# Attention's steps reordered: last keys' scores as steps of their own, steps that run one or two periods late, and the scaling of x on GpSimd throughout

## The chip, the cores and the metric

The kernel runs on one core of one Trainium2 chip. The engines of that core run their own instruction streams side by side and meet through semaphores: TensorE (PE; PEld is its weight load), VectorE (DVE), ScalarE (ACT), GpSimd (POOL) and SyncE (SP), which here issues nearly all DMAs. The metric is the device time of one execution in microseconds. Three runs of the kernel before took 1297.23, 1299.07 and 1300.94 us; the median is 1299.07 us.

## The reference

Two blocks follow each other. The first is attention over 8 batches of 8 heads with 576 positions of 64 values, where a score is kept only if it lies within tau of its row's maximum:

```python
scores = scale * np.matmul(q, k.transpose(0, 1, 3, 2))
thresh = np.max(scores, axis=-1, keepdims=True) - tau
scores = np.where(scores >= thresh, scores, -1000000000.0)
scores = scores - np.max(scores, axis=-1, keepdims=True)
attn = np.exp(scores)
attn = attn / (np.sum(attn, axis=-1, keepdims=True) + 1e-09)
return np.matmul(attn, v).astype(np.float32)
```

Its output, turned into 4608 rows of 512 values, is the x of a feed-forward block:

```python
h = np.maximum(x @ w_in, 0.0)
return (h * h @ w_out).astype(np.float32)
```

w_in is 512 x 2048 and w_out is 2048 x 512. Both arrive as 64-bit floats and the kernel converts them to 32 bits on the chip.

## The kernel before

**Stages.** Attention comes first. The feed-forward block follows, with a fast form of matrix product that trades products for sums (the helpers on lines 121 to 133). The two share TensorE's accumulation memory, PSUM: the feed-forward stage opens its own pools there only when attention's are closed. The conversion of the weights and part of the sums on them are spread over attention's periods.

**Units, pairs and periods.** Two heads make a head pair (32 of them). The queries of a head pair are cut into four blocks of 128; the last 64 queries of two head pairs make a ninth unit. That gives 144 units. `period(p)` (line 619) takes two units, A = 2p and B = 2p + 1; the text calls them pair p. There are 72 such pairs. The loop on line 1146 runs the periods one after the other, and each runs the steps of a list in the order in which the list names them. Since the kernel schedules by hand, this order is also the order of each engine's own stream. `CONVERTING` is the list while weights are converted (periods 2 to 34), `PLAIN` the one after that, and `BEGIN_WITH` holds those of periods 0 and 1.

**The steps and their engines.**

| step | what it does, line | engine |
|---|---|---|
| SA, SB | scores of A, of B against the first 512 keys (L434); SA also does the last 64 keys of both units | PE |
| topA0 ... topB1 | copies 128 x 576 scores out of PSUM and takes their extreme (L452) | DVE |
| leastA, leastB | adds tau (L459) | POOL |
| powA0 ... | exponential (L462) | ACT |
| maskA0 ... | threshold, product and row sum (L467) | DVE |
| over, inv | row sum + 1e-9 (L474), reciprocal (L477), for the pair before | POOL, DVE |
| V, W, U | turn the weights of a pair with transposes (L380), in three parts; W also spreads the reciprocals with small products (L515) | PE |
| eV, eW, eU | copy the turned weights to SBUF (L523) | ACT |
| PV | product of values and weights (L532), 72 or 108 instructions | PE |
| x | takes PV out of PSUM (L657 or L659) | ACT or DVE |
| xm | scales x on GpSimd in converting periods (L669), hands the stores of x and the next loads of v to SP | POOL, SP |
| T, eT | turn queries or keys with transposes (L398), copy them (L403, L411), ask for the next loads | PE, ACT, SP |
| fetch, c1 ... c6 | load a block of weights and convert it: L205 (c1), L212 (c2), L219 (c3), L227 (c4), L235 (c5), L245 (c6) | SP, ACT, POOL, POOL, DVE, DVE, POOL |
| s1, s2 | one sum on the weights each (L122, L125) | POOL |

In period p of the old lists, scores, exponentials and masks are those of pair p, V and W turn pair p - 1, U and PV belong to pair p - 2. The table `TURNS` names the periods in which T has something to turn; of the periods 35 to 71 those are 30.

**PSUM.** Six banks (`sc`) hold scores: A's first 512 keys lie in banks 0 and 5, B's in banks 2 and 3, and the last 64 keys of both in banks 1 and 4. T turns into the free middle of banks 1 and 4 (`spots`), W into banks 2 and 3, PV into banks 0 and 5. Two more banks (`pt`) serve U and V.

**Waits.** `touch` (line 355) notes which banks an instruction uses. To each new one it adds a wait for the last instruction of every other engine on the same bank, and it declares that instructions on other banks don't depend on each other, except for the kinds in `MEET` (line 353) whose ring slots coincide. Rings hold three head pairs of turned queries (`Q_RING`), four of turned keys and of the last queries (`K_RING`), and two pairs of turned weights (`W_RING`).

Of the kernel before, what the change touches and what calls it, by code (L numbers as in the profile page):

```python
# [10 lines left out]
FP32 = mybir.dt.float32  # L11
# [37 lines left out]
def kernel(  # L49
# [300 lines left out]
    behind = mybir.DependencyInfo(mybir.DependencyClass.Sync, mybir.DependencyReason.DATA)  # L350

    Q_RING, K_RING, W_RING = 3, 4, 2
    MEET = (("scores", "turned", (Q_RING, K_RING)), ("values", "weights", (W_RING,)), ("x", "weights", (W_RING,)))

    def touch(what, made, at, size, key=0):

# [34 lines left out]
    def turn(i, which, spots, other=None):  # L391

        nat, to = loaded.pop((i, which)), places(i)
        of = [nat[:, t, :] for t in range(FULL)] + ([loaded.pop((i, 2))] if which else [])
        for t, x in enumerate(of):
            for r, (spot, at) in enumerate(spots):
                rows = ds(r * HALF, HALF)
                made = nc.tensor.transpose(spot[:, ts(t, HALF)], x[rows, :], ident[rows, rows])  # L398
                touch("turns", made, at, BANK)
        half = FULL * HALF  # L400

        def scaled(to, spot):
            touch("turned", nc.scalar.activation(out=to, in_=spot[0], func=AF.Identity, scale=qscale[:, :]), spot[1], BANK, i)  # L403

        def then():
            part = lambda r, x, n: (spots[r][0][:, ds(x, n)], spots[r][1])
            if which:
                for r, n in ((0, half), (1, half + REST)):
                    spot = part(r, 0, n)
                    copy_by = other if r and other else nc.scalar.copy  # L410
                    touch("turned", copy_by(to[1][:, ds(r * half, n)], spot[0]), spot[1], BANK, i)  # L411
# [11 lines left out]
    def scores(n, rest):  # L423

        of, t = units[n]
        at_k, count = (MAIN, REST) if rest else (0, MAIN)
        for j in range(2):
            first = n % 2 != j
            to = (3 * j + 1) * BANK + first * (BANK - REST) if rest else (3 * j + 2 * first) * BANK
            for c in range(2):  # L430
                rows, at = ds(j * D, D), ds(c * HALF, HALF)
                qT, kT, qR = turned[of[c]]
                lhs = qT[rows, ds((c * FULL + t) * HALF, HALF)] if t < FULL else qR[rows, :]
                made = nc.tensor.matmul(  # L434
                    sc[at, ds(to, count)], lhs, kT[rows, ds(at_k, count)], start=True, stop=True
                )
                touch("scores", made, to, count, of[c])

    def softmax(n):

        if n % 2 == 0:
            smalls[n // 2] = sb.tile([P, 4, 4], FP32, tag="small", bufs=4, name="small")
        small = smalls[n // 2]
        nmx, thr, sm = (small[:, i, ds(n % 2 * 2, 2)] for i in range(3))
        w = sb.tile([P, CH, 2, D], FP32, tag="w", bufs=4, name="w")
        s = sb.tile([P, 2, S], FP32, tag="s", bufs=2, name="s")
        weights[n] = w
        of = lambda j: s[:, j, :].rearrange("p (c d) -> p c d", d=D)

        def top(j):  # L450
            at = 3 * j * BANK + (n % 2 != j) * (2 * BANK - REST)
            made = nc.vector.tensor_scalar(  # L452
                out=s[:, j, :], in0=sc[:, ds(at, S)], scalar1=1.0, scalar2=None,
                op0=ALU.mult, op1=ALU.min, accum_out=nmx[:, j : j + 1],
            )
            touch("tops", made, at, S)

        def least():
            nc.gpsimd.tensor_scalar(out=thr, in0=nmx, scalar1=tau_p[:, :], scalar2=None, op0=ALU.add)  # L459

        def power(j):
            nc.scalar.activation(  # L462
                out=w[:, :, j, :], in_=of(j), func=AF.Exp, bias=nmx[:, j : j + 1], scale=-1.0
            )

        def mask(j):
            nc.vector.scalar_tensor_tensor(  # L467
                out=w[:, :, j, :], in0=of(j), scalar=thr[:, j : j + 1], in1=w[:, :, j, :],
                op0=ALU.is_le, op1=ALU.mult, accum_out=sm[:, j : j + 1],
            )  # L470
# [88 lines left out]
    def has(n):  # L559
        return 0 <= n < NU  # L560
# [22 lines left out]
    def converts(p):  # L583
        return is_wide and (has_chunk(p) or has_chunk(p - 1))
# [4 lines left out]
    def begun(n):  # L589
        return starts.get(n)  # L590

    PLAIN = """
        SA c3 T topA0 over U eU s1 SB topA1 powA1 leastA topB0 powB0 c1 s2 PV c4 V fetch
        inv powA0 c5 topB1 powB1 eT maskA1 x xm W eV maskA0 leastB c2 c6 eW maskB0
        maskB1
    """.split()
    CONVERTING = """
        fetch SA U eU T SB topA0 s1 c1 topA1 topB0 c3 V PV leastA over powA0 topB1
        powA1 powB0 c4 eT inv x maskA1 maskA0 W leastB maskB0 c5 eV c2 powB1 c6 eW maskB1 xm
    """.split()  # L600

    BEGIN_WITH = {
        0: """
            SA SB fetch topA0 T topA1 leastA topB0 topB1 leastB powA0 powA1 eT powB0 powB1
            maskA0 maskA1 maskB0 maskB1
        """.split(),
        1: """
            fetch SA SB T eT over topA0 topA1 leastA inv V topB0 topB1 leastB powA0 powA1 eV W
            powB0 eW maskA0 maskA1 powB1 maskB0 maskB1
        """.split(),  # L610
    }

# [6 lines left out]
    def period(p):  # L619
# [30 lines left out]
        def values_out():  # L650
            if not has(2 * m):
                return
            late["x"] = x = sb.tile([P, 2, P], FP32, tag="x", bufs=2, name="x")
            for j in range(2):
                from_ = sc[:, ds(5 * j * BANK, P)]
                if converts(p):
                    made = nc.scalar.copy(x[:, j, :], from_)  # L657
                else:
                    made = nc.vector.tensor_tensor(  # L659
                        out=x[:, j, :], in0=from_, in1=wT[m][:, ts(SCALE_AT + j, P)], op=ALU.mult  # L660
                    )
                touch("x", made, 5 * j * BANK, P, m)

        def given_out():
            if has(2 * m):
                x = late.pop("x")
                if converts(p):
                    both = x[:, :, :].rearrange("p j n -> p (j n)")
                    nc.gpsimd.tensor_tensor(out=both, in0=both, in1=wT[m][:, ds(SCALE_AT * P, 2 * P)], op=ALU.mult)  # L669
                wT.pop(m)  # L670
                valued(m)
                give_x(m, x)
            ask(False)

        def scored_a():
            if has(A):
                scores(A, False)
                scores(A, True)
                scores(B_, True)
                softmax(A)  # L680

        def scored_b():
            if has(A):
                scores(B_, False)
                softmax(B_)

        def every(key):
            for then in late.get(key, ()):
# [27 lines left out]

    def inner(product, copy, temp, bank, final, tick):

# [400 lines left out]
    with tc.manual_schedule():  # L1119
        with ExitStack() as stack:  # L1120
# [222 lines left out]
```

## Time and profile before

| | |
|---|---|
| median of three runs | 1299.07 us |
| span of the profiled execution | 1298.2 us |
| granted TensorE clock, mean | 0.997 |
| PE, DVE, ACT, POOL busy | 98%, 78%, 65%, 71% |
| attention, up to the first product of the feed-forward stage | 507.8 us |

The profile is of one execution, and its sums are made against its span of 1298.2 us, which is 0.9 us under the median. A row of the timeline gives the start, the time, the engine and line, the operation, output and input by the program's names, and a count where several like instructions are merged. A bracket at its end names the idle time before it and what ended that. Instructions of one engine overlap in part, so the distance from one start to the next says what an instruction costs its engine, and the time of one says when its result is there.

### The profile page before, as it was taken

The page shows a single profiled execution, that of the slowest core. Times are in us where ns is not written, and L with a number is a line of the kernel's source. Part 1 is how long each engine was busy: PE and PEld are TensorE (multiplying, and loading weights), DVE is VectorE, ACT ScalarE, POOL GpSimd, SP SyncE. Part 2 cuts the span into 40 slices and gives each one's busy share as a digit, 9 for nine tenths or more (in the row PEclk, how much of TensorE's full clock was granted, in tenths as well). Part 3 has the DMA queues.
Part 4 walks back from the last instruction along what each step waited for, and adds up shares of the span by engine and source line. Part 5 has one row for each costly group of instructions (what it writes and reads, how often), then busy time and mean ns, then how long its engine had stood idle before and what let it go on. Part 6 is the DMA issues. An engine that isn't in the chain of part 4 may idle for free.

```text
span 1298.2 us, 45819 instructions
## 1 busy us (share of the span) xinstructions
PE 1276.4 (98%) x18287; PEld 1117.7 (86%) x18287; DVE 1007.0 (78%) x2423; ACT 845.5 (65%) x1498; POOL 926.8 (71%) x1031
## 2 busy tenths in 40 slices
PE   8999999999999999999999999999999999999998
PEld 5777777677777778988888888999999999999998
DVE  6999999999999996886887878867646654665463
ACT  6999999888998984666765856675523432343240
POOL 2787878755555321888897989858787767777775
PEclk8999999999999999999999999999999999999999
DMA  5665566544333312667768768589554224522411
GB/s 143 163 160 154 153 192 180 149 103 110 85 79 80 92 34 64 191 183 218 212 186 226 218 175 235 162 304 391 195 159 164 83 86 159 163 80 88 160 34 34
DMA packets 291413, 196.20 MB, mean 151 GB/s; under 512 B 100096, under 2 KB 252160, under 8 KB 291200
## 3 DMA queue, kind: packets, MB, share of 16 engines
q1 hardware_dynamic: 289888, 192.87, 51.5%
q8 instruction: 144, 2.36, 0.8%
q14 instruction: 69, 0.57, 0.2%
q10 hardware_dynamic: 1312, 0.41, 0.1%
HBM read 120.85 MB, written 72.35 MB: 149 GB/s over the span
## 4 chain that ended last, share of the span: by engine, by line
PE 86%; ACT 5%; DVE 4%; DMA 3%; issue 2%; POOL 0%; SPq 0%; ACTq 0%; DVEq 0%; POOLq 0%
PE po L1077 28%; PE ph L935 16%; PE sc L532 11%; PE sc L434 10%; PE ph L942 10%; PE pt L380 6%; DVE arena L452 2%; PE sc L515 2%; PE sc L398 2%; ACT arena L462 1%; ACT arena L523 1%; DMA g<-arena 1%; PE sc L380 1%; DVE arena L125 1%; DMA wall<-w 1%
## 5 line engine op out<-in xcount | busy, mean ns | idle before, releaser
L125 POOL TENSOR_TENSOR arena<-arena 128x512 f32<-128x512 f32 (+1 forms) x314 | 378.1, 1222 | 147.0 <-DVE arena L125 119.3
L1077 PE MATMUL po<-wall,arena 128*128 128x128 f32 x3528 | 395.0, 275 | 1.9 <-ACT arena L752 1.4
L1077 PEld LDWEIGHTS po<-wall,arena 128*128 128x128 f32 x3528 | 394.4, 192 | 2.5 <-ACT arena L752 1.8
L125 DVE TENSOR_TENSOR arena<-ph,arena 128x512 f32<-128x512 f32 x378 | 255.1, 689 | 79.9 <-PE ph L935 31.5
L122 POOL TENSOR_TENSOR arena<-arena 128x128 f32<-128x128 f32 (+1 forms) x322 | 265.4, 825 | 23.0 <-DMA arena<-w 6.6
L935 PE MATMUL ph<-arena,wall 128*128 128x256 f32 x1176 | 256.6, 380 | 1.8 <-DVE arena L125 1.4
L935 PEld LDWEIGHTS ph<-arena,wall 128*128 128x128 f32 x1176 | 222.2, 190 | 35.9 <-DVE arena L125 5.4
L125 DVE TENSOR_TENSOR arena<-po,arena 128x128 f32<-128x128 f32 x378 | 108.2, 290 | 167.7 <-PE po L1077 163.4
L467 DVE SCALAR_TENSOR_TENSOR arena<-arena 128x576 f32<-128x576 f32 x288 | 235.7, 855 | 0.9 <-ACT arena L462 0.9
L791 ACT COPY c<-arena 128x512 f32<-128x512 f32 (+1 forms) x295 | 169.0, 578 | 71.8 <-DVE arena L122 35.8
L452 DVE TENSOR_SCALAR_CACHE_REDUCE arena<-sc 128x576 f32<-128x576 f32 x288 | 205.1, 748 | 10.9 <-ACT arena L523 4.3
L462 ACT ACTIVATE arena<-arena 128x576 f32<-128x576 f32 x288 | 208.7, 773 | 7.4 <-DVE arena L452 4.2
L532 PEld LDWEIGHTS sc<-arena 64*64 64x64 f32 x5760 | 159.2, 133 | 36.5 <-DVE arena L452 19.8
L532 PE MATMUL sc<-arena 64*64 64x128 f32 (+1 forms) x5760 | 180.5, 262 | 2.9 <-DVE arena L452 1.3
L434 PE MATMUL sc<-arena 64*64 64x64 f32 (+1 forms) x2304 | 176.2, 415 | 3.8 <-ACT arena L403 2.4
L523 ACT COPY arena<-pt 128x1024 f32<-128x1024 f32 x144 | 146.4, 1016 | 27.9 <-PE pt L380 26.5
L122 DVE TENSOR_TENSOR arena<-arena,c 128x512 f32<-128x512 f32 x235 | 154.4, 666 | 11.0 <-ACT c L791 7.6
L752 ACT COPY arena<-po 128x128 f32<-128x128 f32 x63 | 16.6, 264 | 186.4 <-PE po L1077 183.7
L942 PE MATMUL ph<-arena,wall 128*128 128x128 f32 x1176 | 132.0, 275 | 0.7 <-DVE arena L659 0.7
L942 PEld LDWEIGHTS ph<-arena,wall 128*128 128x128 f32 x1176 | 131.6, 192 | 1.1 <-issue 0.8
L380 PEld LDWEIGHTS pt<-ident,arena 64*128 64x128 f32 x2304 | 83.5, 139 | 40.0 <-ACT arena L523 30.1
L434 PEld LDWEIGHTS sc<-arena 64*64 64x64 f32 x2304 | 74.0, 134 | 42.2 <-issue 14.1
(54 smaller groups left out, 1079.7 us busy)
## 6 DMA issues: line engine op xcount, KB each, us to landing
arena<-g SPq DMA_DIRECT2D x144, 256.0 KB, 4.4
g<-arena SPq DMA_DIRECT2D x192, 128.0 KB, 2.9
w<-arena SPq DMA_DIRECT2D x60, 256.0 KB, 2.8
wall<-w SPq DMA_DIRECT2D x49, 256.0 KB, 5.2
g<-arena SPq DMA_DIRECT2D x48, 256.0 KB, 3.8
arena<-w SPq DMA_DIRECT2D x44, 256.0 KB, 3.3
arena<-in_v_dram SPq DMA_DIRECT2D x32, 288.0 KB, 3.8
out_dram<-arena SPq DMA_DIRECT2D x70, 128.0 KB, 2.2
```

Of the source, the lines that this page charges most:

```text
L122: e.tensor_tensor(out=out, in0=x, in1=y, op=ALU.subtract)
L125: e.tensor_tensor(out=out, in0=x, in1=y, op=ALU.add)
L380: made = nc.tensor.transpose(pt[:, r, ts(slot, HALF)], of[rows, :], ident[rows, rows])
L434: made = nc.tensor.matmul(sc[at, ds(to, count)], lhs, kT[rows, ds(at_k, count)], start=True, stop=True)
L452: made = nc.vector.tensor_scalar(out=s[:, j, :], in0=sc[:, ds(at, S)], scalar1=1.0, scalar2=None, op0=ALU.mult, op1=ALU.min, accum_out=nmx ...
L462: nc.scalar.activation(out=w[:, :, j, :], in_=of(j), func=AF.Exp, bias=nmx[:, j : j + 1], scale=-1.0)
L467: nc.vector.scalar_tensor_tensor(out=w[:, :, j, :], in0=of(j), scalar=thr[:, j : j + 1], in1=w[:, :, j, :], op0=ALU.is_le, op1=ALU.mult, a ...
L532: made = nc.tensor.matmul(sc[ds(u * D, D), ds(5 * j * BANK + row, count)], loaded_v[i][rows, (c - (u != j)) % CH, :], wT[m][rows, ds(weigh ...
L791: nc.scalar.copy(c, y)
L935: nc.tensor.matmul(to[:, 2 * j : 2 * j + 2, :], W_IN[m, k][:, ts(2 * h + j, P)], part_x(steps, k, m), start=(not more and j == 0), stop=Tr ...
L942: nc.tensor.matmul(to[:, j, :], W_IN[m, k][:, ts(j, P)], x, start=(not more and j == 0), stop=True, skip_group_check=True,)
L1077: nc.tensor.matmul(to, g[:, j, :], w[:, j, :], start=(not more and j == 0), stop=(j == 3), skip_group_check=True)
```

## The change

- `BEGIN_WITH`, `PLAIN` and `CONVERTING` get new orders. A name may end in one or two dashes: in iteration p it then stands for that step of period p - 1 or p - 2. `step` runs each step of each period once, and the periods of one step in their order; where a list changes, steps already run are left out. The loop runs three iterations longer, for the late steps.
- The scores of the last 64 keys leave SA and become the steps RA and RB.
- x is always copied out of PSUM by ACT, and xm always scales it on GpSimd; DVE's product on line 659 goes.
- `MEET` tells turned queries from turned keys and the last queries' scores from the others, so that each is tested against its own ring.
- The buffers for w and s are found by the unit's number instead of by the order of asking.

```diff
-    MEET = (("scores", "turned", (Q_RING, K_RING)), ("values", "weights", (W_RING,)), ("x", "weights", (W_RING,)))
+    MEET = (("scores", "turnedq", (Q_RING,)), ("scores", "turnedk", (K_RING,)), ("last scores", "turnedk", (K_RING,)), ("values", "weights", (W_RING,)), ("x", "weights", (W_RING,)))
...
-        half = FULL * HALF
+        half, kind = FULL * HALF, "turnedk" if which else "turnedq"
...
-                touch("scores", made, to, count, of[c])
+                touch("scores" if t < FULL else "last scores", made, to, count, of[c])
...
-        if n % 2 == 0:
+        if n // 2 not in smalls:
...
-        w = sb.tile([P, CH, 2, D], FP32, tag="w", bufs=4, name="w")
-        s = sb.tile([P, 2, S], FP32, tag="s", bufs=2, name="s")
+        w = sb.tile([P, CH, 2, D], FP32, tag=f"w{n % 4}", name="w")
+        s = sb.tile([P, 2, S], FP32, tag=f"s{n % 2}", name="s")
...
+    FIRST_PERIOD = -2
     PLAIN = """
-        SA c3 T topA0 over U eU s1 SB topA1 powA1 leastA topB0 powB0 c1 s2 PV c4 V fetch
-        inv powA0 c5 topB1 powB1 eT maskA1 x xm W eV maskA0 leastB c2 c6 eW maskB0
-        maskB1
+        PV-- x-- V-- eV-- RA- c1- c3- inv-- W-- xm-- eW-- powB1-- c2 maskA0-- SA- maskA1-- U- c4 topA0- s1--
+        powB0-- topA1- leastA- SB- eU- maskB1-- c6 RB- T- s2 maskB0-- eT- over- topB0- powA0- topB1- c5
+        powA1- leastB- fetch
     """.split()
     CONVERTING = """
-        fetch SA U eU T SB topA0 s1 c1 topA1 topB0 c3 V PV leastA over powA0 topB1
-        powA1 powB0 c4 eT inv x maskA1 maskA0 W leastB maskB0 c5 eV c2 powB1 c6 eW maskB1 xm
+        RB- maskA0-- SA- maskA1-- inv-- powB1-- W-- U- topA0- eW-- c6- fetch topA1- leastA- SB- maskB0-- c1-
+        c3- eT- maskB1-- topB0- c4 over- topB1- c2- leastB- eU- powA1- powA0- PV- c5 V- x- RA powB0- eV- T
+        xm- s1 s2
     """.split()
...
-            SA SB fetch topA0 T topA1 leastA topB0 topB1 leastB powA0 powA1 eT powB0 powB1
-            maskA0 maskA1 maskB0 maskB1
+        SA RA RB SB fetch topA0 T topA1 leastA topB0 topB1 leastB powA0 powA1 eT powB0 powB1 maskA0 maskA1
+        maskB0 maskB1
...
-                if converts(p):
-                    made = nc.scalar.copy(x[:, j, :], from_)
-                else:
-                    made = nc.vector.tensor_tensor(
-                        out=x[:, j, :], in0=from_, in1=wT[m][:, ts(SCALE_AT + j, P)], op=ALU.mult
-                    )
-                touch("x", made, 5 * j * BANK, P, m)
+                touch("x", nc.scalar.copy(x[:, j, :], from_), 5 * j * BANK, P, m)
...
-                if converts(p):
-                    both = x[:, :, :].rearrange("p j n -> p (j n)")
-                    nc.gpsimd.tensor_tensor(out=both, in0=both, in1=wT[m][:, ds(SCALE_AT * P, 2 * P)], op=ALU.mult)
+                both = x[:, :, :].rearrange("p j n -> p (j n)")
+                nc.gpsimd.tensor_tensor(out=both, in0=both, in1=wT[m][:, ds(SCALE_AT * P, 2 * P)], op=ALU.mult)
...
-        def scored_a():
-            if has(A):
-                scores(A, False)
-                scores(A, True)
-                scores(B_, True)
-                softmax(A)
-
-        def scored_b():
-            if has(A):
-                scores(B_, False)
-                softmax(B_)
+        def scored(n):
+            if has(n):
+                scores(n, False)
+                softmax(n)
+
+        def scored_rest(n):
+            if has(n):
+                scores(n, True)
...
-            "SA": scored_a, "SB": scored_b,
+            "SA": lambda: scored(A), "SB": lambda: scored(B_),
+            "RA": lambda: scored_rest(A), "RB": lambda: scored_rest(B_),
...
+        return steps
+
+    tables, made_steps = {}, set()
+
+    def step(name, p):
+
+        if p < FIRST_PERIOD or (name, p) in made_steps:
+            return
+        step(name, p - 1)
+        made_steps.add((name, p))
+        if p not in tables:
+            tables[p] = period(p)
+        tables[p][name]()
+
+    def run_period(p):
+
         for name in BEGIN_WITH.get(p) or (CONVERTING if converts(p) else PLAIN):
-            steps[name]()
-        for n in (A, B_):
-            if has(n) and units[n][1] == FULL:
-                for i in units[n][0]:
-                    turned.pop(i)
+            step(name.rstrip("-"), p - name.count("-"))
...
-            for p in range(-2, NU // 2 + 3):
-                period(p)
+            for p in range(FIRST_PERIOD, NU // 2 + 6):
+                run_period(p)
```

More of the change, by code (lines that the diff above doesn't have):

```diff
@@ L399, in turn @@
                 touch("turns", made, at, BANK)
-        half = FULL * HALF
+        half, kind = FULL * HALF, "turnedk" if which else "turnedq"
         def scaled(to, spot):
-            touch("turned", nc.scalar.activation(out=to, in_=spot[0], func=AF.Identity, scale=qscale[:, :]), spot[1], BANK, i)
+            touch(kind, nc.scalar.activation(out=to, in_=spot[0], func=AF.Identity, scale=qscale[:, :]), spot[1], BANK, i)
         def then():
@@ L410, in then @@
                     copy_by = other if r and other else nc.scalar.copy
-                    touch("turned", copy_by(to[1][:, ds(r * half, n)], spot[0]), spot[1], BANK, i)
+                    touch(kind, copy_by(to[1][:, ds(r * half, n)], spot[0]), spot[1], BANK, i)
                 scaled(to[2], part(0, half, REST))
@@ L603 @@
         0: """
-            SA SB fetch topA0 T topA1 leastA topB0 topB1 leastB powA0 powA1 eT powB0 powB1
-            maskA0 maskA1 maskB0 maskB1
+        SA RA RB SB fetch topA0 T topA1 leastA topB0 topB1 leastB powA0 powA1 eT powB0 powB1 maskA0 maskA1
+        maskB0 maskB1
         """.split(),
         1: """
-            fetch SA SB T eT over topA0 topA1 leastA inv V topB0 topB1 leastB powA0 powA1 eV W
-            powB0 eW maskA0 maskA1 powB1 maskB0 maskB1
+        fetch SA RA RB SB T eT over topA0 topA1 leastA inv V topB0 topB1 leastB powA0 powA1 eV W powB0 eW
+        maskA0 maskA1 powB1 maskB0 maskB1
         """.split(),
```

## The prediction

> **What bounds the kernel now.** I read the page first, then the busy times of stretches, then the order of TensorE's instructions in single periods, then the other engines beside it. The change touches only the attention stage, so the stretches are cut there: the first covers the converting periods between the first score read of pair 2 and of pair 33 (31 periods), the second the plain periods between those of pair 34 and pair 71 (37 periods), the third the drain up to the last read of attention's PSUM.
>
> ```profile
> PE 1276.4 (98%) x18287; PEld 1117.7 (86%) x18287; DVE 1007.0 (78%) x2423; ACT 845.5 (65%) x1498; POOL 926.8 (71%) x1031
> 22.80:243.50 220.70, 216.86 (x5314) 162.04 (x5312) 219.41 (x588) 212.72 (x381) 174.88 (x215) 1.00 0.62 164
> 250.50:493.70 243.20, 240.02 (x6328) 180.41 (x6322) 234.59 (x704) 217.75 (x339) 120.81 (x171) 1.00 0.36 84
> 493.70:507.60 13.90, 12.00 (x374) 9.94 (x368) 7.49 (x26) 8.84 (x11) 1.48 (x4) 1.00 0.13 24
> ```
>
> After the length, the columns are PE, PEld, DVE, ACT and POOL. A converting period lasts 220.7/31 = 7.12 us and DVE is busy 99.4% of it. A plain period lasts 243.2/37 = 6.57 us, with PE at 98.7%, DVE at 96.5%, ACT at 89.5%, POOL at 49.7%. A busy PE need not be a full PE, so one plain period follows, step by step, PE alone (start, length, line, output, count). The last four rows are PVs of two other periods and what follows them.
>
> ```profile
> 372.82 0.71 PE L380 MATMUL pt<-ident,arena 64*128 64x64 f32 x16
> 373.37 0.29 PE L380 MATMUL sc<-ident,arena 64*128 64x64 f32 x4
> 373.59 0.46 PE L515 MATMUL sc<-ident,arena 64*64 64x64 f32 x16
> 373.87 1.27 PE L434 MATMUL sc<-arena 64*64 64x512 f32 x24
> 375.07 0.47 PE L398 MATMUL sc<-ident,arena 64*128 64x64 f32 x8
> 375.38 0.71 PE L380 MATMUL pt<-ident,arena 64*128 64x64 f32 x16
> 376.02 1.09 PE L434 MATMUL sc<-arena 64*64 64x512 f32 x8
> 376.93 0.78 PE L532 MATMUL sc<-arena 64*64 64x128 f32 x14
> ...
> 298.14 2.31 PE L532 MATMUL sc<-arena 64*64 64x128 f32 x72
> 300.38 0.72 PE L380 MATMUL pt<-ident,arena 64*128 64x64 f32 x16
> ...
> 389.90 2.54 PE L532 MATMUL sc<-arena 64*64 64x128 f32 x108
> 392.37 0.71 PE L380 MATMUL pt<-ident,arena 64*128 64x64 f32 x16
> ```
>
> These are V, W's transposes, W's reciprocals, SA with all last keys, T, U, SB, PV. Starts, not lengths, give the costs, as the lengths overlap. From V to PV 376.93 - 372.82 = 4.11 us, and PV without a wait 300.38 - 298.14 = 2.24: 6.35 us with a turn T, and 6.04 without (T takes 375.38 - 375.07 = 0.31). So 6.57 is PE's own work plus 0.23 us of waits (30 of 37 periods have a T: mean work 6.29, to which the eight PVs of a last block add 392.37 - 389.90 - 2.24 = 0.23 each). The waits are PV behind DVE's reads of the same banks, and now and then SA behind ACT. In plain periods PE is the bound.
>
> **PE: the price of a new order.** Two kinds of PE work alternate: transposes on 64*128 tiles and products on 64*64 tiles. A converting period has the same steps with other neighbours:
>
> ```profile
> 142.10 0.41 PE L398 MATMUL sc<-ident,arena 64*128 64x64 f32 x8
> 142.44 1.09 PE L434 MATMUL sc<-arena 64*64 64x512 f32 x8
> 143.46 0.71 PE L380 MATMUL pt<-ident,arena 64*128 64x64 f32 x16
> 144.10 2.85 PE L532 MATMUL sc<-arena 64*64 64x128 f32 x108
> 146.89 0.34 PE L380 MATMUL sc<-ident,arena 64*128 64x64 f32 x4
> 147.16 0.38 PE L515 MATMUL sc<-ident,arena 64*64 64x64 f32 x9
> ```
>
> Sixteen transposes take 0.55 us when transposes follow (372.82 to 373.37) and 0.64 when products follow (375.38 to 376.02, 143.46 to 144.10). SB's eight products take 0.91 when products follow (376.02 to 376.93) and 1.02 when transposes follow (142.44 to 143.46). W's four transposes take 0.22 after transposes, 0.27 after products (146.89 to 147.16). So leaving a kind costs 0.10 us and entering the other some 0.03 to 0.05: about 0.28 for a round trip. The old plain order makes two round trips (SA | T U | SB PV | V W | reciprocals). The new one runs PV | V | RA | W | reciprocals SA | U | SB RB | T |: four with a T, three without. Its sum from the rows: PV 2.24; V 0.64; RA 0.26 (eight of 16 like products, which take 0.28 from 373.59 to 373.87, plus leaving); W's transposes 0.27; reciprocals 0.28; SA 0.97 (the 1.02 less entering); U 0.64; SB 0.91; RB 0.23 (0.12 plus leaving); T 0.40 (0.34 plus entering; 0.06 more for a key turn): 6.84 to 6.90 with a T, say 6.84 as neighbours' ends round down; 6.31 without T and RB's leaving. Over 37 periods, 30 with a T: 30 x 6.84 + 7 x 6.31 + 8 x 0.23 = 251.2 us, against 243.2: **+8.0 us, with no wait left at all**. The waits that the change removes (PV behind the score reads; SA behind a turn of another ring slot, next row) are counted as gone in it.
>
> ```profile
> 288.52 0.21 PEld L434 LDWEIGHTS sc<-arena 64*64 64x64 f32 x8 [0.55 <-ACT arena L403]
> ```
>
> This price bears on a page of the Trainium skill. "TensorEngine Tiling (Array Packing)", Key Properties, says that changing the tiling mode, not merely the tile, drains TensorE. The gaps above agree with its direction at 0.10 us a change and a slower start. The skill's "TensorE: Matmul & The Clock Gate", Single matmul latency, puts a drain at about 175 ns; by that figure, an estimate, each extra round trip would cost 0.35 instead of 0.28, and the total would be some 5 us higher. The rows have the same thing measured, so I keep 0.28.
>
> **A wait that the change adds on PE: RB.** B's last keys go to banks 1 and 4, which A's score reads (topA0, topA1) also cover; the helper that notes banks makes a later PE write wait for the last DVE read of the bank. In the old order both units' last keys stood inside SA, ahead of topA0. Now RB stands behind SB and ahead of T, so T, then the next period's PV, V and RA queue behind it.
>
> ```profile
> 375.65 0.76 DVE L452 TENSOR_SCALAR_CACHE_REDUCE arena<-sc 128x576 f32<-128x576 f32 x1
> 376.34 0.75 DVE L452 TENSOR_SCALAR_CACHE_REDUCE arena<-sc 128x576 f32<-128x576 f32 x1
> ```
>
> SA lasts 1.09 (376.02 above); topA0 starts about 0.07 later, topA1 0.69 after it and lasts 0.75; with another 0.07 RB may write bank 4 some 2.67 us after SA's start. PE reaches RB after SA, U and SB: 0.97 + 0.64 + 0.91 = 2.52. The wait is 0.15 us each period, 37 x 0.15 = **+5.6 us**; its ends are 0 (the two 0.07 are my reading of semaphore delays, and the reads may start on the first half) and 0.25 (a read pushed back by a mask). I take 0.15, which the rows give. The loop T, eT, topB0, topB1, next RA is near it: 0.52 + 0.9 + 1.5 + 3.55 and delays, about 6.9, so it adds nothing yet.
>
> **x on ACT and GpSimd in plain periods.**
>
> ```profile
> 372.93 0.49 DVE L659 TENSOR_TENSOR arena<-sc,arena 128x128 f32<-128x128 f32 x2
> 139.82 0.43 ACT L657 COPY arena<-sc 128x128 f32<-128x128 f32 x2
> 28.75 0.73 POOL L669 TENSOR_TENSOR arena<-arena 128x256 f32<-128x256 f32 x1
> 28.97 1.13 DVE L467 SCALAR_TENSOR_TENSOR arena<-arena 128x576 f32<-128x576 f32 x1 [0.61 <-ACT arena L462]
> ```
>
> DVE loses 0.49 (0.41 from start to start), ACT gains 0.43, POOL 0.73 per period. ACT goes from 5.88 to 6.3 and POOL from 3.3 to 4.0, both below PE's 6.84; DVE falls from 6.34 to about 5.9. I cost all of it at 0: PE covers it. Without that cover, ACT's 6.3 would be the next bound. The last two rows show the other side: a mask that starts while GpSimd scales x takes 1.13 instead of 0.81; DVE's spare 0.9 us covers one such mask.
>
> **Converting periods.** DVE is the bound there, and it pays for GpSimd's port use:
>
> ```profile
> 146.51 2.03 POOL L212 TENSOR_SCALAR arena<-arena 128x512 int32<-128x512 uint32 x1
> 147.00 1.20 DVE L467 SCALAR_TENSOR_TENSOR arena<-arena 128x576 f32<-128x576 f32 x1
> 148.12 0.81 DVE L467 SCALAR_TENSOR_TENSOR arena<-arena 128x576 f32<-128x576 f32 x1
> 148.86 0.68 DVE L235 SCALAR_TENSOR_TENSOR arena<-arena 128x512 int32<-128x512 int32 x1
> ```
>
> Each period one mask beside c2 takes 1.20. The new order starts c2 behind "over", beside the reads of scores, c4 and c5, and moves xm and c6 beside maskA0 and maskA1. If no DVE instruction pays there, DVE needs 7.07 - 0.39 = 6.7 and PE binds: four round trips with nearly the plain order's sum, 6.86. That gains (7.12 - 6.86) x 31 = 8 us. If xm delays maskA1 by 0.32 and c4 pays 0.4 besides, the period is 6.7 + 0.7 = 7.4 or 9 us more. The rows have a slowed mask beside both c2 and xm, and in the new order at least one mask again starts beside xm or c6, so I take no change: **0, between -8 and +9**. The skill's "GPSIMD Engine Reference" says that GpSimd shares its SBUF interfaces with VectorE and contends with instructions that have two SBUF inputs; that speaks for the upper end, and the 0.81 mask beside the same c2 shows it isn't paid by every one.
>
> **Moved DMAs, buffers, start and end.** xm takes its stores and v loads to SP later, but together with the PV that frees and uses them; eT asks for keys and queries two head pairs ahead, some 4 periods or 26 us, against a landing of 3 to 5:
>
> ```profile
> arena<-in_v_dram SPq DMA_DIRECT2D x32, 288.0 KB, 3.8
> 504.64 2.39 PE L532 MATMUL sc<-arena 64*64 64x128 f32 x108
> 507.12 0.49 DVE L659 TENSOR_TENSOR arena<-sc,arena 128x128 f32<-128x128 f32 x2 [4.33 <-issue]
> ```
>
> I count 0 for it, as for the finer ring test and the fixed w and s slots beyond the removed waits. At the start iteration 2 has almost no work and pair 2's scores come no later: 0. The drain has three PVs after pair 71's first score read, before and after, but V, W and U of the last pair now come a full iteration after its masks; following the last evictions one after the other (eV 0.9, eW 0.6, eU 1.0 between three fills, PV, x) I get 15.2 us in place of 13.9: **+1.3**, between 0 and +3. The feed-forward stage starts on the freed PSUM and is PE-bound to the end; it moves as a block.
>
> **Sum.** 8.0 + 5.6 + 0 + 1.3 = +15 us on the profiled execution: 1298.2 goes to 1313. The median of the runs is 0.9 above that span, so 1314.
>
> **Rivals.**
> 1. Forecast: kinds of PE work and RB's wait, converting periods unchanged: 1314, its own range 1307 to 1320.
> 2. Converting periods shed the slowed mask and fall to 6.86: 1314 - 8 = 1306. For: c2 leaves the masks. Against: xm and c6 go to them.
> 3. More masks or c4 pay for GpSimd there, 7.4 us: 1323. For: the 1.13 and 1.20 rows. Against: GpSimd has room to wait instead.
> 4. The other side: a change of kind costs nothing when it stands alone, as the short steps (RA, W, RB) drain in the shadow of what PE would wait for anyway. Then plain periods fall to PE's 6.35: (6.57 - 6.35) x 37 = 8 us less, 1.3 more for the drain, no RB wait: 1292. It decides at about 0.11 us per round trip, in place of the 0.25 that the two sums come to: the 67 extra ones (30 x 2 + 7) then cost 7.3, as much as the waits that go (37 x 0.23 = 8.6) less the drain. For: PE had waits in the old order. Against: the same gaps in every row above.
> 5. The shorter waits and the longer order cancel (RB without a wait and half of rival 2): 1304 or less, no measurable change.
>
> **Chances.** Forecast 0.50, second 0.15, third 0.15, fourth 0.12, fifth 0.08. No change means within 0.3% (3.9 us), about what a measurement of this kernel can tell. That gives 0.12 faster, 0.08 same, 0.80 slower. The range 1300 to 1326 leaves out the fourth and the far end of the third.
>
> **What would show it.** After: PE's start-to-start sums of 6.8 to 7.0 us in plain periods with a T, with the gap at each change of kind; RB's weight loads idle behind DVE's score reads; DVE under 92% there, ACT at 93% or less; converting periods at 7.0 to 7.2 with one mask of over 1.1 us. The prediction is wrong if plain periods are under 6.6 (price of a change of kind), if PE idles for long behind ACT (a loop that I missed), or if converting periods leave 7.0 to 7.2.

## The result, and the profile after

The changed kernel takes 1318.52 us (median of four runs, 1316.80 to 1319.72) against 1298.15 us (median of four runs of the kernel before, 1297.05 to 1300.94). The measured ratio is 1.0149 with a 95% interval of 1.0132 to 1.0167; the quotient of the two medians is 1.0157 and lies inside it. It is 1.5% slower. The profiled execution has a span of 1315.0 us, 16.8 us over the span before, and the comparison of the stages uses these two spans. The medians differ by 20.4 us: the profiled execution of the changed kernel is the quickest of its four, so some 3.6 us of the difference are not in the stages below. Two executions behind this document, the profiled one of rb_early (1732.86 us) and one of conv_kinds (1588.83 us), ran at a granted clock of 0.68 and 0.75 and count in no median here.

The same three stretches of attention follow from the changed kernel, cut at the same score reads (length; then the busy time of PE, PEld, DVE, ACT and POOL; then clock, DMA share, GB/s):

```profile
22.40:245.20 222.80, 217.17 (x5288) 149.83 (x5288) 211.31 (x585) 207.34 (x378) 200.55 (x216) 1.00 0.62 163
252.80:507.80 255.00, 254.91 (x6336) 184.05 (x6336) 218.77 (x630) 231.09 (x411) 194.33 (x205) 1.00 0.34 78
507.80:522.70 14.90, 12.47 (x388) 10.45 (x387) 7.64 (x22) 10.85 (x19) 4.10 (x7) 1.00 0.16 30
```

By the starts that the table below uses, the plain stretch is 11.8 us longer (255.0 against 243.2), the converting one 2.2, the drain 0.9, and the passage between the two lists 0.5 (7.58 against 7.05 us from pair 33's first score read to pair 34's); the time up to pair 2's first score read is 0.4 shorter. In the plain stretch PE is now busy to 99.96% (a figure that counts the short waits at single products as busy), while DVE has fallen from 96.5% to 85.8%. The relief of DVE is there, and it buys nothing, because PE's own list has grown. The feed-forward stage takes 1.8 us more:

```profile
507.80:1298.20 790.40, 783.02 (x5880) 747.98 (x5880) 526.19 (x1054) 387.56 (x735) 620.92 (x624) 1.00 0.55 170
```

```profile
522.70:1315.00 792.30, 783.38 (x5880) 747.87 (x5880) 526.75 (x1054) 388.01 (x735) 621.43 (x625) 1.00 0.55 170
```

The first of these rows is of before, the second of after: the same work, with 1.5 us more of PE idle.

PE's order in a plain period of the changed kernel (timeline, PE alone):

```profile
330.70 2.19 PE L532 MATMUL sc<-arena 64*64 64x128 f32 x72
332.83 0.71 PE L380 MATMUL pt<-ident,arena 64*128 64x64 f32 x16
333.47 0.34 PE L434 MATMUL sc<-arena 64*64 64x64 f32 x8
333.75 0.34 PE L380 MATMUL sc<-ident,arena 64*128 64x64 f32 x4
334.01 0.46 PE L515 MATMUL sc<-ident,arena 64*64 64x64 f32 x16
334.30 1.04 PE L434 MATMUL sc<-arena 64*64 64x512 f32 x8
335.27 0.71 PE L380 MATMUL pt<-ident,arena 64*128 64x64 f32 x16
335.91 1.37 PE L434 MATMUL sc<-arena 64*64 64x512 f32 x16
337.21 0.46 PE L398 MATMUL sc<-ident,arena 64*128 64x64 f32 x8
337.60 2.33 PE L532 MATMUL sc<-arena 64*64 64x128 f32 x108
```

The steps are PV, V, RA, W's transposes, the reciprocals with SA, U, SB with RB, T and the next PV. From PV to PV it is 337.60 - 330.70 = 6.90 us. The 64*64 and 64*128 rows alternate eight times: four round trips, where the old order had two. SB and RB together (335.91 to 337.21) take 1.30 us; without a wait they would take 0.91 + 0.23 = 1.14. The waits of the plain stretch name what RB waits for:

```profile
PEld sc L434 <- DVE arena L452: 8.0, 29, 0.3
```

That is one wait of weight loads for score reads in each of the 29 periods between 288 and 488 us, 0.28 us each at PEld, of which some 0.15 reach the products.

### The profile page after: what moved, and what is told of

It reads as the page before. It is cut to its first block, busy times and chain, and to the rows that moved or that the text cites. A ratio compares the mean times of both kernels' runs of the same rounds, so it can differ in the third digit from the quotient of the medians.

```text
span 1315.0 us, 46033 instructions
## 1 busy us (share of the span) xinstructions
PE 1292.6 (98%) x18287; PEld 1108.5 (84%) x18287; DVE 983.6 (75%) x2345; ACT 856.6 (65%) x1576; POOL 1030.5 (78%) x1070
## 4 chain that ended last, share of the span: by engine, by line
PE 54%; DMA 3%; ACT 2%; DVE 1%; issue 1%; SPq 1%; POOL 0%; ACTq 0%; DVEq 0%; POOLq 0%
PE po L1082 28%; PE ph L940 15%; PE ph L947 10%; DVE arena L125 1%; DMA g<-arena 1%; DMA wall<-w 1%; ACT c L796 1%; DMA arena<-xT 1%; SPq L778 1%; ACT arena L909 0%; DMA w<-arena 0%; ACT arena L910 0%; DVE arena L122 0%; PE sc L532 0%; ACT arena L523 0%
## 5 line engine op out<-in xcount | busy, mean ns | idle before, releaser
L452 DVE TENSOR_SCALAR_CACHE_REDUCE arena<-sc 128x576 f32<-128x576 f32 x288 | 208.4, 753 | 51.0 <-ACT arena L523 36.3
L467 DVE SCALAR_TENSOR_TENSOR arena<-arena 128x576 f32<-128x576 f32 x288 | 223.1, 811 | 1.1 <-ACT arena L462 1.1
L462 ACT ACTIVATE arena<-arena 128x576 f32<-128x576 f32 x288 | 213.3, 784 | 3.2 <-DVE arena L452 3.2
L434 PE MATMUL sc<-arena 64*64 64x512 f32 (+1 forms) x2304 | 195.6, 423 | 4.6 <-ACT arena L403 0.7
L532 PEld LDWEIGHTS sc<-arena 64*64 64x64 f32 x5760 | 148.6, 133 | 28.5 <-issue 13.0
L459 POOL TENSOR_SCALAR arena<-arena,tau_p 128x2 f32<-128x2 f32 x144 | 102.8, 714 | 87.2 <-DVE arena L452 56.6
L532 PE MATMUL sc<-arena 64*64 64x128 f32 (+1 forms) x5760 | 166.0, 262 | 2.6 <-ACT arena L523 0.8
```

The source lines that it names most:

```text
L434: made = nc.tensor.matmul(sc[at, ds(to, count)], lhs, kT[rows, ds(at_k, count)], start=True, stop=True)
L452: made = nc.vector.tensor_scalar(out=s[:, j, :], in0=sc[:, ds(at, S)], scalar1=1.0, scalar2=None, op0=ALU.mult, op1=ALU.min, accum_out=nmx ...
L462: nc.scalar.activation(out=w[:, :, j, :], in_=of(j), func=AF.Exp, bias=nmx[:, j : j + 1], scale=-1.0)
L467: nc.vector.scalar_tensor_tensor(out=w[:, :, j, :], in0=of(j), scalar=thr[:, j : j + 1], in1=w[:, :, j, :], op0=ALU.is_le, op1=ALU.mult, a ...
L532: made = nc.tensor.matmul(sc[ds(u * D, D), ds(5 * j * BANK + row, count)], loaded_v[i][rows, (c - (u != j)) % CH, :], wT[m][rows, ds(weigh ...
```

## The experiments

Eleven more kernels were run. Theory K is the prediction's: changes between the two kinds of PE work, and RB's wait, make the plain periods longer. The stage times below are worked out from the starts of the first score read of pairs 2, 33, 34 and 71, and of the first feed-forward product, in each profile.

| kernel | median us | converting | plain | drain | feed-forward |
|---|---|---|---|---|---|
| before | 1298.15 | 220.6 | 243.2 | 14.0 | 790.4 |
| after | 1318.52 | 222.8 | 255.0 | 14.9 | 792.3 |
| ra_beside_sa | 1308.49 | 223.6 | 245.5 | 14.9 | 792.8 |
| plain_kinds | 1314.81 | 222.9 | 254.1 | 14.9 | 790.4 |
| old_conv | 1311.18 | 219.9 | 255.4 | 14.9 | 790.0 |
| x_on_dve | 1334.43 | 224.1 | 271.6 | 15.1 | 791.9 |
| conv_kinds | 1311.68 | 215.7 | 255.5 | 14.9 | 793.5 |
| x_alone | 1343.99 | 220.1 | 288.9 | 14.0 | 789.3 |
| rb_early_old_conv | 1297.39 | 219.6 | 242.3 | 14.9 | 789.1 |
| x_least_first | 1321.34 | 219.7 | 266.9 | 14.4 | 790.5 |
| x_least_x_first | 1307.60 | 219.5 | 252.3 | 14.0 | 789.6 |
| both_early | 1296.40 | 214.9 | 241.5 | 14.9 | 792.0 |

The eleventh, rb_early, has a median of 1303.88 us and no stage times that can be compared.

### One round trip taken away: ra_beside_sa

```diff
-        PV-- x-- V-- eV-- RA- c1- c3- inv-- W-- xm-- eW-- powB1-- c2 maskA0-- SA- maskA1-- U- ...
+        PV-- x-- V-- eV-- c1- c3- inv-- W-- xm-- eW-- powB1-- c2 maskA0-- RA- SA- maskA1-- U- ...
```

> Edit: in the plain list of the changed kernel RA moves from behind V to just ahead of SA; nothing else. TensorE then makes three round trips between its two kinds of work in a plain period with a turn, in place of four. Theory K (changes of kind and RB's wait): the start-to-start sum of a period falls from 6.96 to about 6.71 us, 37 x 0.25 = 9 us less, 1309 us. Rival A (the ACT chain sets the period: topB0 waits for eT, 22.3 us in 28 waits in the changed kernel, and x was put on ACT): TensorE only waits elsewhere, under 2 us of change, 1317 to 1319.

Measured: 1308.49 us (ratio to before 1.0076, 1.0061 to 1.0091), 10.0 us less for one name moved in a list. The rival that gave the time to ACT's chain falls. A period of this kernel, PE alone:

```profile
404.57 0.71 PE L380 MATMUL pt<-ident,arena 64*128 64x64 f32 x16
405.12 0.29 PE L380 MATMUL sc<-ident,arena 64*128 64x64 f32 x4
405.34 0.46 PE L515 MATMUL sc<-ident,arena 64*64 64x64 f32 x16
405.62 1.16 PE L434 MATMUL sc<-arena 64*64 64x64 f32 x16
406.71 0.71 PE L380 MATMUL pt<-ident,arena 64*128 64x64 f32 x16
```

V takes 0.55 instead of 0.64 and W's transposes 0.22 instead of 0.26, as they are neighbours again; RA and SA together take 1.09 instead of 0.28 + 0.97. The instructions are the same, and a period falls by 0.30 us: from 6.96 to 6.66 with ten transposes in T, from 6.90 to 6.60 with eight. The round trip cost 0.30.

### The old order of PE in the new plain list: plain_kinds

```diff
-  ... eV-- RA- c1- ... maskA0-- SA- maskA1-- U- ... c6 RB- T- s2 ...
+  ... eV-- c1- ... maskA0-- RA- RB- SA- maskA1-- T- U- ... c6 s2 ...
```

> Edit: in the plain list of the changed kernel RA and RB stand ahead of SA, and T between SA and U, as in the old order of TensorE; all steps keep their lateness, the other engines their order. Theory K: two round trips and no wait of RB, so a plain period falls to TensorE's own work of some 6.3 us plus small waits, say 6.4: 37 x (6.89 - 6.4) = 18 us less, about 1300 us. Rival A: ACT's chain keeps the period over 6.7, so 1311 or more. Rival L (the deeper lateness itself costs, by loops between the engines): also over 1311.

Measured: 1314.81 us (1.0125, 1.0108 to 1.0142), only 3.7 us less, and only 0.9 us in the plain stretch. Theory K fails here: PE's work fell, but its idle time took its place, and rival L was right for this order. DVE's rows of one period, then PE's, show the loop:

```profile
409.22 0.75 DVE L452 TENSOR_SCALAR_CACHE_REDUCE arena<-sc 128x576 f32<-128x576 f32 x1
...
412.36 0.76 DVE L452 TENSOR_SCALAR_CACHE_REDUCE arena<-sc 128x576 f32<-128x576 f32 x1 [0.84 <-ACT arena L462]
...
413.04 0.75 DVE L452 TENSOR_SCALAR_CACHE_REDUCE arena<-sc 128x576 f32<-128x576 f32 x1
...
413.71 0.81 DVE L467 SCALAR_TENSOR_TENSOR arena<-arena 128x576 f32<-128x576 f32 x1
...
414.45 0.81 DVE L467 SCALAR_TENSOR_TENSOR arena<-arena 128x576 f32<-128x576 f32 x1
...
415.43 0.76 DVE L452 TENSOR_SCALAR_CACHE_REDUCE arena<-sc 128x576 f32<-128x576 f32 x1 [0.15 <-DVE arena L467]
...
416.12 0.75 DVE L452 TENSOR_SCALAR_CACHE_REDUCE arena<-sc 128x576 f32<-128x576 f32 x1
```

```profile
410.03 0.33 PE L380 MATMUL sc<-ident,arena 64*128 64x64 f32 x3 [0.19 <-DVE arena L452]
410.29 0.46 PE L515 MATMUL sc<-ident,arena 64*64 64x64 f32 x16
410.57 1.27 PE L434 MATMUL sc<-arena 64*64 64x64 f32 x24
411.78 0.46 PE L398 MATMUL sc<-ident,arena 64*128 64x64 f32 x8
412.08 0.66 PE L380 MATMUL pt<-ident,arena 64*128 64x64 f32 x16
```

W waits for topB1, as both use banks 2 and 3; RA, RB, SA and T follow; topA0 starts when T has ended, as it reads bank 1; two masks and topB0 stand between it and the next topB1. From 409.22 to 416.12 that is 6.90 us, the period. The profile puts topA0's idle time down to ACT, which had ended another instruction just then; T's end (411.78 + 0.46 = 412.24) fits as well and is in the loop of banks. The run's own periods without a turn speak for T: there topA0 starts 0.11 us behind SA's end (362.48 + 1.27 = 363.75), and the period is 6.48 us instead of 6.90.

```profile
362.48 1.27 PE L434 MATMUL sc<-arena 64*64 64x64 f32 x24
...
363.86 0.76 DVE L452 TENSOR_SCALAR_CACHE_REDUCE arena<-sc 128x576 f32<-128x576 f32 x1 [0.44 <-ACT arena L523]
```

With ten transposes in T instead of eight the period is 6.97. The next run took T out of that loop.

### RB ahead of SA, T behind SB: rb_early

```diff
-  ... maskA0-- RA- SA- ... c6 RB- T- s2 ...      (of ra_beside_sa)
+  ... maskA0-- RA- RB- SA- ... c6 T- s2 ...
```

> Edit: in the plain list of the changed kernel RA and RB both stand ahead of SA; T stays behind SB, all else too. Against the run with RA alone beside SA (1308.5), RB no longer waits behind topA0 and topA1. Theory K: the 0.15 us of that wait goes in every plain period, with a little more as T meets what is left of it: a period with a turn falls from 6.66 to about 6.5, one without from 6.37 to about 6.1, together 37 x 0.18 = 7 us less, 1302 us. Rival W (the wait is only handed on to T): under 2 us less, 1307 or more. Rival L (a loop through W, SA, the score reads and masks back to W): a floor near 6.9 as with T ahead of U, so more than 1308.

Measured: 1303.88 us (1.0039, 1.0024 to 1.0053), 4.6 us under ra_beside_sa. Theory K expected 7 and rival W under 2. The same plain list in rb_early_old_conv has periods of 6.48 to 6.63 us, with and without a turn, but for three of 6.83 to 6.86, so PE is no longer the only bound: the periods without a turn got longer (6.37 to 6.48) while those with one got shorter (6.66 to 6.51). RB's wait is gone. Without a turn this list is that of plain_kinds, and the period is the same 6.48 us; so the loop above, without T, is likely what is left, though no run breaks it.

### The converting list: old_conv and conv_kinds

old_conv puts the old converting list back:

```diff
-        RB- maskA0-- SA- maskA1-- inv-- powB1-- W-- U- topA0- eW-- c6- fetch ...
+        fetch SA RA RB U eU T SB topA0 s1 c1 topA1 topB0 c3 V PV leastA over powA0 topB1 ...
```

> Edit: the converting list of the changed kernel goes back to the old order (RA and RB right behind SA, no step late); the plain list stays new. Theory K: only the converting part of the loss comes back, 31 x (7.19 - 7.12) = 2 us, perhaps 1 more at the passage between the lists where pipelines fill: 1315 to 1319, plain periods still 6.9 to 7.0. A rival that puts the loss on the converting periods' lateness and DMA times: over 8 us less, under 1310.

Measured: 1311.18 us (1.0102, 1.0087 to 1.0117), 7.3 us less: neither theory's number. The stages of the two profiles account for 5.8: 2.9 in the converting stretch, 0.5 at the passage, 2.3 in the feed-forward stage.

conv_kinds keeps the new list and moves RA behind T, so that V and T, and RA, RB and SA, are neighbours:

```diff
-        ... PV- c5 V- x- RA powB0- eV- T
+        ... PV- c5 V- x- powB0- eV- T RA
```

> Edit: in the converting list of the changed kernel RA moves behind T, so that V and T stand side by side and RA, RB, SA too; the plain list stays as changed. Theory K: one round trip less in the 28 converting periods with a turn, 28 x 0.28 = 8 us less, 1310 us. Rival A (SB's wait behind eW and PV's behind eU set the period there): under 2 us less, 1316 or more.

Measured: 1311.68 us (1.0088, 1.0065 to 1.0111), 6.8 us less where theory K expected 8. From V to W's transposes, PE alone, in the changed kernel and in conv_kinds:

```profile
142.38 0.71 PE L380 MATMUL pt<-ident,arena 64*128 64x64 f32 x16
143.02 0.34 PE L434 MATMUL sc<-arena 64*64 64x64 f32 x8
143.29 0.46 PE L398 MATMUL sc<-ident,arena 64*128 64x64 f32 x8
143.69 1.21 PE L434 MATMUL sc<-arena 64*64 64x64 f32 x16
144.82 0.34 PE L380 MATMUL sc<-ident,arena 64*128 64x64 f32 x4
```

```profile
140.04 0.71 PE L380 MATMUL pt<-ident,arena 64*128 64x64 f32 x16
140.59 0.41 PE L398 MATMUL sc<-ident,arena 64*128 64x64 f32 x8
140.93 1.32 PE L434 MATMUL sc<-arena 64*64 64x64 f32 x24
142.19 0.34 PE L380 MATMUL sc<-ident,arena 64*128 64x64 f32 x4
```

The first takes 2.44 us, the second 2.15. Converting periods with a turn fall from 7.26 to 6.96 us, 0.30 again, and are now shorter than the old list's 7.07. So what PE saves shortens the new converting periods too; the waits that PE has there did not take it up.

### Where x is made: x_on_dve and x_alone

x_on_dve gives DVE its product back in the new order. x_alone does this part of the change alone in the old order.

```diff
 x_alone, against before:
-                if converts(p):
-                    made = nc.scalar.copy(x[:, j, :], from_)
-                else:
-                    made = nc.vector.tensor_tensor(
-                        out=x[:, j, :], in0=from_, in1=wT[m][:, ts(SCALE_AT + j, P)], op=ALU.mult
-                    )
+                touch("x", nc.scalar.copy(x[:, j, :], from_), 5 * j * BANK, P, m)
...
 x_on_dve, against after: the reverse
```

> Edit: in plain periods x is made by DVE again, in one product out of PSUM, as in the kernel before; the rest is the changed kernel. Theory K: TensorE's order is the same, so the time stays within 2 us of the changed kernel's 1318.5. Rival A: ACT gets 0.43 us per plain period back and the time falls by 8 us or more, to under 1311.

> Edit: the kernel before with one part of the change alone: x is copied by ACT and scaled by GpSimd in all periods; orders as before. Theory K: TensorE binds the plain periods, so the time stays within 3 us of 1298. Rival A (ACT's added copies cost): 37 x 0.3 = 11 us more or over. Rival D (DVE is the bound in plain periods): 37 x 0.4 = 15 us less.

Measured: x_on_dve 1334.43 us (1.0280, 1.0265 to 1.0295), 15.9 more than after; x_alone 1343.99 us (1.0345, 1.0329 to 1.0360), 45.8 more than before. Every theory missed both. In x_alone the waits are led by a pair that the kernel before doesn't have, and one period's rows show the queue:

```profile
DVE arena L467 <- POOL arena L459: 40.7, 23, 2.1
```

```profile
385.43 0.43 ACT L656 COPY arena<-sc 128x128 f32<-128x128 f32 x2
...
385.94 0.74 POOL L662 TENSOR_TENSOR arena<-arena 128x256 f32<-128x256 f32 x1 [2.11 <-ACT arena L656]
...
386.65 0.30 POOL L459 TENSOR_SCALAR arena<-arena,tau_p 128x2 f32<-128x2 f32 x1
...
386.98 0.82 DVE L467 SCALAR_TENSOR_TENSOR arena<-arena 128x576 f32<-128x576 f32 x1 [1.79 <-POOL arena L459]
```

x waits on ACT behind eT; xm waits on GpSimd for x, 2.11 us; leastB, a 0.30 us instruction that could have run long before, stands behind xm; and DVE's maskB0 waits 1.79 us for leastB. In x_on_dve it is the meeting of masks and GpSimd's sums:

```profile
407.77 1.27 POOL L122 TENSOR_TENSOR wall<-wall 128x512 f32<-128x512 f32 x1
407.82 1.84 DVE L467 SCALAR_TENSOR_TENSOR arena<-arena 128x576 f32<-128x576 f32 x1
```

A mask that starts 0.05 us after a sum on GpSimd takes 1.84 us in place of 0.81. Between 330 and 480 us this befalls 20 of 80 masks, one in each period; masks average 1050 ns there, against 808 ns in the changed kernel, and DVE, with x back, is busy 97% of the time (145.29 of 150 us). That this is the whole of the 15.9 us is argued from these rows; no run takes the meeting away. So x on ACT and GpSimd belongs to the new order, and the new order to it.

### x_alone mended: x_least_first and x_least_x_first

```diff
-        inv powA0 c5 topB1 powB1 eT maskA1 x xm W eV maskA0 leastB c2 c6 eW maskB0
+        inv powA0 c5 topB1 leastB powB1 eT maskA1 x xm W eV maskA0 c2 c6 eW maskB0     (x_least_first)
+        inv powA0 c5 topB1 leastB powB1 x eT maskA1 xm W eV maskA0 c2 c6 eW maskB0     (x_least_x_first)
```

> Edit: the kernel with x alone changed (1344.0), and leastB moved in the plain list from behind xm to right behind topB1, so that it stands ahead of xm in GpSimd's queue. Theory Q (the loss of that kernel is leastB queued behind xm, which waits for ACT's copy of PV, while maskB0 waits for leastB: 1.8 us in each plain period): about 37 x 1.2 = 44 us less, 1300, with a remainder where SA waits for x behind eT (0.3 to 0.4 us a period, so up to 1306). Rival A (ACT's and GpSimd's added work costs by itself): still over 1325.

> Edit: as x_least_first, and the copy x stands ahead of eT in ACT's queue, so that SA, which reuses the banks of PV, doesn't wait for it. TensorE keeps the two round trips of the old order. Theory K with Q: TensorE's own 6.3 us a plain period and little else, 6.35 to 6.5: 37 x 0.1 to 0.2 = 3 to 8 us under the kernel before, 1290 to 1296. If PV's wait for the score reads stays as it was: 1297 to 1300.

Measured: 1321.34 us (1.0176, 1.0162 to 1.0189) and 1307.60 us (1.0064, 1.0052 to 1.0077). leastB's place was worth 22.7 us and x's place 13.7 more. Both queue positions are thus shown as causes, but each was worth less, or left more, than expected: the second kernel is still 9 us over before, and what makes up these 9 us is open (its masks average 932 ns between 330 and 480 us, against 815 before). In the first, SA still waits behind x:

```profile
400.33 1.47 PE L434 MATMUL sc<-arena 64*64 64x512 f32 x24 [0.57 <-ACT arena L656]
```

### The two mended lists together: both_early and rb_early_old_conv

both_early has the plain list of rb_early and the converting list of conv_kinds; rb_early_old_conv has the same plain list and the old converting list.

> Edit: the changed kernel with both mended lists: RA and RB ahead of SA in plain periods (1304.0 by itself, 14.5 less), RA behind T in converting periods (1312.1 by itself, 6.4 less). Theory K: the two add up, since each takes round trips from its own periods: 1297 to 1298, as long as the kernel before within 0.3%. If they share a cause: over 1300.

> Edit: the plain list with RA and RB ahead of SA, and the converting list in the old order. If the two effects add (7 us less for the old converting list, 1311.2 in place of 1318.5, and what RA and RB beside SA give): about 1295 us, under the kernel before. If the old converting list's gain lay in how the new plain list meets it: 1298 or more.

Measured: both_early 1296.40 us (ratio to before 0.9982, 0.9973 to 0.9991), rb_early_old_conv 1297.39 us (0.9992, 0.9983 to 1.0001). The two mends are worth 14.6 and 6.8 alone and 22.1 together: they add. both_early is the only kernel of the study under the kernel before by more than its interval, by 0.2%, and it differs from the changed kernel in the place of three names.

## Why the prediction was right

It forecast 1314 us, +15, by changes of kind and RB's wait; 1318.5 was measured, +16.8 on the profiled execution. The plain stretch and the drain, which the forecast was summed from, came to +12.7 us in place of the 14.9 predicted; the other 4.1 lie in stretches that it put at 0, so that the total comes so near is in part luck.

- **PE's longer list: +8.0 predicted, and +5.6 for RB's wait; +11.8 measured for the two.** Step by step the sums hold: V 0.64 (0.64 predicted), RA 0.28 (0.26), W's transposes 0.26 (0.27), reciprocals 0.29 (0.28), SA 0.97 (0.97), U 0.64 (0.64), SB with RB and its wait 1.30 (0.91 + 0.23 + 0.15), T 0.39 (0.40). PV was mis-sized: 2.13 in place of 2.24, where I had taken a PV of the old order as free of waits. It has one: in the kernel before, PV's weight loads wait for DVE's score reads in every plain period (this row is from 310 to 460 us), and in the changed kernel's plain stretch that wait is gone.

```profile
PEld sc L532 <- DVE arena L452: 6.7, 23, 0.3
```

  In the single instructions of the PV at 298.14, the second product starts 0.11 us behind the first; in the changed kernel's at 330.70 the first four start within 0.02. That is about 0.11 x 37 = 4 us too much in the sum. The longer PVs of a last block add 0.13 instead of 0.23 (339.86 - 337.60 = 2.26), another 0.8 too much; smaller steps go the other way, such as the turns with ten transposes at 0.46 in place of 0.40. Nearly all periods have 6.90 or 6.96 with a turn, 7.03 to 7.07 with a last block's PV too, and 6.51 without a turn, against a predicted 6.99 to 7.05, some 7.25 and 6.46; one of 7.42 stands out. ra_beside_sa shows the price of a round trip as 0.30, where the rows had given 0.28.
- **RB's wait.** 0.15 predicted, 1.30 - 1.14 = 0.16 measured.
- **x on ACT and GpSimd at 0.** The measured kernel agrees: by its busy time PE idles 0.1 us in the whole plain stretch, and its regular wait, RB's, is for DVE. But the sentence that PE covers it rested on engine totals. x_alone moves the same work and loses 46 us, 36 of them through the places of x and leastB in two queues. The cover is the new order, with PV and x at a period's start, not PE's load.
- **Converting periods at 0.** 222.8 against 220.6 us is near it, for other reasons than given. "At least one mask again starts beside xm or c6" failed: the masks take 0.81 and 0.82, and GpSimd waits in their place, as rival 3's "against" had it:

```profile
139.84 0.82 DVE L467 SCALAR_TENSOR_TENSOR arena<-arena 128x576 f32<-128x576 f32 x1
...
140.05 1.08 POOL L219 TENSOR_SCALAR arena<-arena 128x512 f32<-128x512 f32 x1
...
143.69 0.81 DVE L467 SCALAR_TENSOR_TENSOR arena<-arena 128x576 f32<-128x576 f32 x1
...
143.89 1.20 POOL L664 TENSOR_TENSOR arena<-arena 128x256 f32<-128x256 f32 x1
```

  DVE's share falls to 211.31/222.80 = 94.8%, as rival 2 needed; yet the periods didn't fall to 6.86, as SB now waits behind eW, with only U between W and SB to cover it:

```profile
139.05 0.21 PEld L434 LDWEIGHTS sc<-arena 64*64 64x64 f32 x8 [0.26 <-ACT arena L523]
```

  PE's work without waits, step by step, is 6.79 us, near the predicted 6.86; U with SB's wait behind it takes 0.83 instead of 0.64, and PV, which waits as well, 2.42 instead of 2.13. That makes 7.26 us. The term came out right by luck, because two errors met in it.
- **Drain.** +1.3 predicted, +0.9 measured.
- **Feed-forward, moved as a block: 0 predicted, +1.8 measured.** The five profiles with the old converting list besides before's have 789.1 to 790.5 us there, the six with the new one, after's among them, 790.4 to 793.5. So it may go with that list, but the two groups overlap by 0.1 us, each kernel has one profile, and what in the list would do this is open.
- **Rivals.** The fourth (a change of kind costs nothing alone) falls with ra_beside_sa and conv_kinds: 0.30 us per round trip in both. The second and third fall with the masks above: the slowed mask did go, yet the periods stayed, and no mask or c4 paid for GpSimd but one mask of 1.27 us and one c4 of 0.80. The fifth falls too, as RB waits and the converting periods give nothing back.

## What to carry to other kernels

When a schedule is reordered, count what the new neighbours cost on the engine that binds, here the changes between transposes and products on TensorE, before counting what other engines save. A step moved to a less busy engine is not free because that engine has room: list what stands behind it in that engine's queue, and who waits for that. Three orders of the same work, x_alone and its two mends, differed by up to 36 us here, and one name moved back in the changed kernel was worth 10.

## What the runs showed of the hardware

- Changing between products on 64*64 tiles and transposes on 64*128 tiles costs TensorE about 0.30 us per round trip (6.96 to 6.66 in plain periods, 7.26 to 6.96 in converting ones, the same instructions). In this kernel every transpose has the one tile shape and every product the other, so the runs don't tell whether the shape or the operation costs. The Trainium skill's "TensorEngine Tiling (Array Packing)", Key Properties, says that a change of mode drains TensorE; these runs agree with it and put a number to it. The number is under the estimate of 0.35 that the prediction made from the 175 ns of the Trainium skill's "TensorE: Matmul & The Clock Gate", Single matmul latency.
- Where a GpSimd instruction and a mask on DVE overlap, the one that starts second can take longer: a mask that starts 0.05 us after a GpSimd sum of 1.27 us takes 1.84 in place of 0.81; xm, starting 0.20 us after a mask, takes 1.20 in place of 0.73. It is not a full exclusion: in the kernel before, the mask at 147.00 took 1.20 us and ended inside the c2 that had started at 146.51 and took 2.03. No mask of the kernel before took over 1.30 us.
